# Interleaving the wo and w4 projections, and their loads, with the last batch's PV in a decode-attention kernel

## Chip, cores, metric

One core of one Trainium2 chip. The metric is the device time of one execution in microseconds. The kernel before takes 239.89 us (median of 4 runs, 239.72 to 240.89). Profiled spans start and end inside that time: the run profiled for the kernel before has a span of 238.0 us.

The engines are PE (TensorE, matmuls), PEld (its weight loads), DVE (VectorE), ACT (ScalarE), POOL (GpSimd) and SP (SyncE, which issues the loads here). The granted clock is the share of TensorE's full clock that it was given. PV is the product of the softmax weights and V; wo, w3 and w4 stand for the matmuls with these weights. A hand-over is the time in which PE waits until DVE has copied a result that PE's next matmuls read.

## The reference, cut to what matters

```python
def reference(A_x, A_k_cache, A_v_cache, A_wq, A_wo, B_x, B_w1, B_w2, B_w3, B_w4):
    x = A_x                                     # 4 x 1 x 576
    xn = _layernorm(x)
    return x + attention(xn, ...) + mixer_mlp(xn, ...)

# attention: 4 batches, 32 query heads on 16 K/V heads, the last 2048 of 8192 keys, head size 128
    q = xn @ wq;  p = softmax(q k^T * Dh**-0.5);  o = p v;   return o @ wo     # wo: 4096 x 576
# mixer_mlp with one token: its shifted groups are all padding, so x1 = xn
    h2 = gelu(layernorm(xn) @ w3) @ w4;         return xn + h2                 # w3: 576 x 4608, w4: 4608 x 576
```

About three quarters of the traffic is K and V, 32 loads of 1 MB for each of the two; the four weights add some 20 MB. 87.17 MB are read in all.

## The kernel before

K is transposed on TensorE, scores are built from 2-column matmuls, and PV runs in batches of four K/V heads: 16 accumulating matmuls of 512 columns. A "group" is two heads, one V load. The last batch, b = 3, holds groups 24 to 31. The parts that the change touches:

```python
def pe_PVbatch(b, gg):                      # 16 matmuls, 128x512, into one of two PSUM banks
    n = b * NPB + gg
    for G in range(pr0 // GP, (pr0 + PVB) // GP):
        PE.wait(("vld", G))                 # both V groups have landed
    ...
def pv_evac(b, gg):                         # DVE: four 128x128 evictions, scaled by 1/sum
    ...
def pe_oTacc(b, gg):                        # PE: transposing matmuls, 128 columns, all heads accumulate
    PE.op(... e.matmul(out=misc[:, OTF:OTF + 128], lhsT=otmp[:, j, :], rhs=imask[:, j, :], start=first, stop=last))
# ... cut
for g in range(NGB):                        # groups of a batch, here as they run for the last one
    dma_kv("v", b * NGB + g)
    if ((g + 1) * GP) % PVB == 0:
        gg = ((g + 1) * GP) // PVB - 1
        if gg >= 1:
            pe_oTacc(b, gg - 1)
        pe_PVbatch(b, gg)
        pv_evac(b, gg)
    if not nxt:
        for j in w3_after.get(g, []):       # w3 blocks 0..3 in groups 0, 2, 4, 6
            dma_w3(j)
            pe_h2T(j)
pe_oTacc(b, NPB - 1)
DVE.op(... e.tensor_copy(out=oT_sb[..., b], in_=misc[:, OTF:OTF + HQ]))
# ... after the last batch
for i in range(len(w4_blocks)):             # blocks of 10, 9, 9, 5, 2, 1 chunks
    dma_w4(i)
for h in range(HQ):                         # wo: 32 heads x 5 matmuls of 4 columns
    ...
for i, (region, f0, n) in enumerate(w4_blocks):
    PE.wait(("w4", i))
    for fc in range(f0, f0 + n):            # w4: 36 chunks x 5 matmuls of 4 columns
        # the last of the five reads 64 columns into the next chunk, so it must have landed too
        if REM > 0 and fc + 1 < FC and w4_blocks[blk_of_fc[fc + 1]][0] == region:
            PE.wait(("w4", blk_of_fc[fc + 1]))
        ...
```

All loads go out from one queue (SyncE's), in program order; PE runs in program order as well.

## Time and profile before

| | before |
|---|---|
| median time | 239.89 us |
| profiled span | 238.0 us |
| last V group landed, PV starts | 215.6 us |
| last transfer ends | about 229 us |
| last w4 matmul done | 234.4 us |

The prediction below shows the page's slices, the chain and the timeline. One more view is useful for the comparison: what PE waited for from 183 us on, in the kernel before (engine, line, what it waited for: us in total, times, longest).

```profile
PE ktp L564 <- DMA wA<-in_B_w_dram: 5.3, 4, 1.9
PE pvb_ps L512 <- DMA v_ring<-in_A_v_cache_dram: 3.2, 4, 1.0
...
PE st_ps L702 <- issue: 1.2, 2, 0.8
...
PE st_ps L687 <- DVE oT_sb L672: 0.3, 1, 0.3
```

PE waits for transfers in small pieces, up to the last V group. After it no wait is for a transfer. DVE is listed with one wait of 0.3 us ahead of wo, but the way from the end of PV (221.94) to wo (223.71) took 1.8 us in all, with DVE's evictions and PE's transposing matmuls in turn. A line such as L687 names where in the code the instruction comes from (wo); L702 is w4, L564 is w3, L512 is PV.

### The profile page before, as it was taken

How to read it: one execution, taken by the hardware profiler on the slowest of the kernel's cores; microseconds unless marked ns; L12 is line 12 of the kernel's file. 1: busy time of each engine (PE TensorE's matmuls, PEld its weight loads, DVE VectorE, ACT ScalarE, POOL GpSimd, SP SyncE). 2: the span in 40 equal slices, each digit the busy share in tenths (PEclk: the TensorE clock that was granted, in tenths of full speed). 3: DMA queues.
4: the chain of work that ended last, by engine and by line, in shares of the span. 5: the costliest groups of instructions: out<-in, count | busy, mean ns of one | idle time of the engine just before them, and what ended most of it. 6: DMA issues, size and time to landing. Idle time of an engine off the chain costs nothing.

```text
span 238.0 us, 6574 instructions
## 1 busy us (share of the span) xinstructions
PE 193.9 (81%) x3071; PEld 149.0 (63%) x3075; DVE 86.1 (36%) x195; ACT 63.8 (27%) x67; POOL 5.4 (2%) x9
## 2 busy tenths in 40 slices
PE   0499697779999697799998859999893758688884
PEld 0399597676867566767866557867662433333583
DVE  4444234542644426533644442635435010110200
ACT  8135143532423331333423043324313000000000
POOL 8000000000000000000000000000000000000000
PEclk9999769956999997799999957999999597675755
DMA  5999999999999999999999999999999999999910
GB/s 192 381 372 379 392 356 395 409 410 407 405 409 408 400 407 408 409 406 408 412 405 398 412 405 410 409 406 410 399 394 338 378 350 351 368 340 358 367 60 4
DMA packets 31240, 87.61 MB, mean 368 GB/s; under 512 B 1496, under 2 KB 10220, under 8 KB 31212
## 3 DMA queue, kind: packets, MB, share of 16 engines
q1 hardware_dynamic: 31212, 87.19, 96.7%
q8 instruction: 24, 0.39, 0.7%
q14 instruction: 4, 0.03, 0.0%
HBM read 87.17 MB, written 0.00 MB: 366 GB/s over the span
## 4 chain that ended last, share of the span: by engine, by line
PE 47%; DMA 34%; SPq 8%; DVE 7%; issue 2%; ACT 1%
PE ktp L440 18%; PE pvb_ps L512 15%; DMA k_ring<-in_A_k_cache_dram 14%; DMA v_ring<-in_A_v_cache_dram 12%; SPq L265 8%; DMA wA<-in_A_wq_dram 7%; PE st_ps L481 5%; DVE otmp L528 2%; PE st_ps L702 2%; DVE kt_sb L453 2%; PE st_ps L687 2%; PE misc_ps L549 2%; DVE part_sb L642 1%; ACT kt_sb L458 1%; DVE pm_sb L604 1%
## 5 line engine op out<-in xcount | busy, mean ns | idle before, releaser
L440 PE MATMUL ktp<-ident_bf,k_ring 128*128 128x128 bf16 x1024 | 89.1, 239 | 5.7 <-DMA k_ring<-in_A_k_cache_dram 3.7
L458 ACT ACTIVATE kt_sb<-ktp 128x1024 bf16<-128x1024 bf16 x51 | 52.1, 1023 | 93.5 <-PE ktp L440 93.5
L440 PEld LDWEIGHTS ktp<-ident_bf,k_ring 128*128 128x128 bf16 x1024 | 69.5, 108 | 8.5 <-DMA k_ring<-in_A_k_cache_dram 4.2
L512 PE MATMUL pvb_ps<-v_ring,pT_sb 128*128 128x512 bf16 x256 | 67.0, 421 | 3.2 <-DMA v_ring<-in_A_v_cache_dram 3.2
L453 DVE COPY kt_sb<-ktp 128x1024 bf16<-128x1024 bf16 x77 | 52.4, 690 | 42.4 <-PE ktp L440 42.3
L512 PEld LDWEIGHTS pvb_ps<-v_ring,pT_sb 128*128 128x128 bf16 x256 | 26.3, 106 | 37.3 <-issue 16.3
L481 PE MATMUL st_ps<-qT_sb,kt_sb 128*128 128x2 bf16 x1024 | 44.6, 165 | 1.8 <-ACT kt_sb L458 1.4
L528 DVE TENSOR_SCALAR otmp<-pvb_ps,rrs 128x128 bf16<-128x128 f32 x64 | 18.0, 343 | 75.7 <-PE pvb_ps L512 75.7
L481 PEld LDWEIGHTS st_ps<-qT_sb,kt_sb 128*128 128x128 bf16 x1024 | 40.4, 99 | 4.0 <-ACT kt_sb L458 1.7
L564 PE MATMUL ktp<-uT_sb,wA 128*128 128x4 bf16 x180 | 5.3, 165 | 5.3 <-DMA wA<-in_B_w_dram 5.3
L549 PE MATMUL misc_ps<-imask,otmp 128*128 128x128 bf16 x64 | 8.7, 231 | 1.0 <-DVE otmp L528 0.4
L564 PEld LDWEIGHTS ktp<-uT_sb,wA 128*128 128x128 bf16 x180 | 5.0, 100 | 6.8 <-DMA wA<-in_B_w_dram 6.3
L613 ACT ACTIVATE pT_sb<-st_ps 128x512 bf16<-128x512 f32 x4 | 2.4, 597 | 24.8 <-PE ktp L440 17.7
L569 ACT ACTIVATE gT_sb<-ktp 128x36 bf16<-128x36 f32 x4 | 0.8, 200 | 30.0 <-PE ktp L564 30.0
L645 PE MATMUL misc_ps<-ones_f,part_sb 128*128 128x1 f32 x8 | 2.1, 337 | 7.3 <-DVE part_sb L642 7.3
L336 PE MATMUL misc_ps<-ident_bf,xn_pad 128*128 128x128 bf16 x5 | 0.7, 302 | 7.6 <-DVE xn_pad L319 7.6
L549 PEld LDWEIGHTS misc_ps<-imask,otmp 128*128 128x128 bf16 x64 | 4.5, 100 | 3.4 <-DVE otmp L528 3.4
L645 PEld LDWEIGHTS misc_ps<-ones_f,part_sb 128*128 128x128 f32 x8 | 1.8, 280 | 6.8 <-DVE part_sb L642 6.8
L336 PEld LDWEIGHTS misc_ps<-ident_bf,xn_pad 128*128 128x128 bf16 x5 | 0.5, 130 | 7.5 <-issue 7.5
L702 PE MATMUL st_ps<-gT_sb,k_ring 128*128 128x4 bf16 x140 | 4.2, 166 | 1.2 <-issue 1.2
L702 PEld LDWEIGHTS st_ps<-gT_sb,k_ring 128*128 128x128 bf16 x140 | 4.0, 104 | 1.4 <-issue 1.4
L687 PE MATMUL st_ps<-oT_sb,wo_sb 128*128 128x4 bf16 x160 | 4.4, 166 | 0.3 <-DVE oT_sb L672 0.3
(68 smaller groups left out, 51.6 us busy)
## 6 DMA issues: line engine op xcount, KB each, us to landing
k_ring<-in_A_k_cache_dram SPq DMA_DIRECT2D x32, 1024.0 KB, 15.2
v_ring<-in_A_v_cache_dram SPq DMA_DIRECT2D x32, 1024.0 KB, 16.9
wo_sb<-in_A_wo_dram SPq DMA_DIRECT2D x4, 1152.0 KB, 19.2
wA<-in_B_w_dram SPq DMA_DIRECT2D x4, 1152.0 KB, 16.1
wA<-in_A_wq_dram SPq DMA_DIRECT2D x4, 1024.0 KB, 12.1
k_ring<-in_B_w_dram SPq DMA_DIRECT2D x2, 1296.0 KB, 16.3
k_ring<-in_B_w_dram SPq DMA_DIRECT2D x1, 1440.0 KB, 19.2
kt_sb<-in_B_w_dram SPq DMA_DIRECT2D x1, 720.0 KB, 11.2
```

What stands on the lines that cost most here:

```text
L265: DQ.ops.append(("op", lambda e, o=out_ap, i=in_ap, s=s: e.dma_start(o, i).then_inc(s, 16), False))
L440: PE.op(lambda e, tt=tt, t=t, src=src, bank=bank: e.transpose(out=bank[:, tt * 128:(tt + 1) * 128], in_=src[:, t * 128:(t + 1) * 128], ide ...
L453: DVE.op(lambda e: e.tensor_copy(out=dst, in_=src), mark=("evac", c))
L458: ACT.op(lambda e: e.activation(out=dst, in_=src, func=ACTF.Copy), mark=("evac", c))
L481: PE.op(lambda e, t=t, src=src, hl0=hl0, b=b, stb=stb, st0=(first_of_b and tt == 0): e.matmul(out=stb[:, t * HL + hl0:t * HL + hl0 + REP], ...
L512: PE.op(lambda e, t=t, vs0=vs0, bank=bank: e.matmul(out=bank[:, 0:PVB * 128], lhsT=pT_sb[:, t, :], rhs=v_ring[:, vs0:vs0 + PVB, t * 128:(t ...
L528: DVE.op(lambda e, jj=jj, j=j, bank=bank: e.tensor_scalar(out=otmp[:, j, :], in0=bank[:, jj * 128:(jj + 1) * 128], scalar1=rrs32[:, 0:1], ...
L549: PE.op(lambda e, j=j, first=first, last=last: e.matmul(out=misc[:, OTF:OTF + 128], lhsT=otmp[:, j, :], rhs=imask[:, j, :], start=first, s ...
L564: PE.op(lambda e, ff=ff, fc=fc, dc=dc, bank=bank: e.matmul(out=bank[:, ff * B:(ff + 1) * B], lhsT=wA[:, dc, fc * 128:(fc + 1) * 128], rhs= ...
L645: PE.op(lambda e: e.matmul(out=misc[:, RSC:RSC + 1], lhsT=part_sb[:, :], rhs=ones_f[:, 0:1], start=True, stop=True), mark=("rs", b))
L687: PE.op(lambda e, h=h, dc=dc, c0=c0: e.matmul(out=accT[:, dc * B:(dc + 1) * B], lhsT=wo_sb[:, h * D + c0:h * D + c0 + 128], rhs=oT_sb[:, h ...
L702: PE.op(lambda e, fc=fc, dc=dc, c0=c0, last=last: e.matmul(out=accT[:, dc * B:(dc + 1) * B], lhsT=w4_chunk(fc, c0, 128), rhs=gT_sb[:, fc * ...
```

## The change

The intent: while the last batch still waits for V, PE should already do the wo matmuls of finished heads and the w4 matmuls. For this the oT matmuls write only the columns of their own heads, with one DVE copy per PV batch; the last PV batch of four heads is split into two halves; the loads of w4 are moved up between V groups; and x's load and half of the output go out from ACT's queue.

```diff
+    for b_ in range(B):
+        for gg_ in range(NPB):
+            if b_ == B - 1 and gg_ == NPB - 1 and PVB > GP:
+                for k_ in range(PVB // GP):
+                    PVBATCH.append((b_, gg_ * PVB + k_ * GP, GP))      # two half batches
+            else:
+                PVBATCH.append((b_, gg_ * PVB, PVB))
...
+        act_dma(x_sb[:, :], A_x.rearrange("b s d -> (b s) d"), s_x, key="x")
...
+        def pe_oTacc(n):
+            for jj in range(npr):
+                PE.op(... out=misc[:, OTF + c0:OTF + c1], lhsT=otmp[:, j, :], rhs=imask[:, j, c0:c1],
+                    start=(jj == 0), stop=(jj == npr - 1)) ...
+            DVE.op(... e.tensor_copy(out=oT_sb[...][:, c0:c1, b], in_=misc[:, OTF + c0:OTF + c1]), mark=("oTb", n))
...
+                extra = [("w3", j) for j in range(NWB)] + [("w4", i) for i in range(len(w4_blocks))]
+                n_tail = max(1, min(3, len(w4_blocks) - 1))
+                mid = extra[:len(extra) - n_tail]       # w3 x4, w4[10], w4[9], w4[9]: one in each of groups 0..6
+                tail = extra[len(extra) - n_tail:]      # w4[5], w4[2], w4[1]
...
+                for g in range(NGB):
+                    dma_kv("v", b * NGB + g)
+                    for n in batches:
+                        if (j0 + npr) == (g + 1) * GP:
+                            pe_PVbatch(n)
+                            pv_evac(n)
+                            flush_pending()             # oT matmuls and wo of the batch before
+                            pending.append(n)
+                    for item in per_g.get(g, []):
+                        do_extra(item)                  # load w3/w4 block, then its matmuls
+                for k, item in enumerate(tail):
+                    if k == 1 or k == len(tail) - 1:
+                        flush_pending()
+                    do_extra(item)
-        for i in range(len(w4_blocks)):
-            dma_w4(i)
-        for h in range(HQ):  ...                        # wo, then w4, after everything
...
-            tiny_dma(out2[:, NFULL * 128:D], out20[NFULL * B:NR, 0:REM], s_out)
+            ACT.wait("fin")
+            act_dma(out2[:, NFULL * 128:D], out20[NFULL * B:NR, 0:REM], s_out)
```

More of the change, by code (lines that the diff above doesn't have):

```diff
@@ L110, in bass_parallel_sum__sliding_block_cached__mixer_s_mlp__decode_kernel @@
     NPB = HKV // PVB
+    PVBATCH = []
+    for b_ in range(B):
[5 more added lines that the diff above has]
+                PVBATCH.append((b_, gg_ * PVB, PVB))
+    PVB_OF_B = {b_: [n_ for n_, (bb_, _, _) in enumerate(PVBATCH) if bb_ == b_] for b_ in range(B)}
     TPC = min(8, NT)
@@ L267, in bass_parallel_sum__sliding_block_cached__mixer_s_mlp__decode_kernel, with act_dma @@
         tiny_dma = sp_dma
+        def act_dma(out_ap, in_ap, s, key=None):
+            dma_counts[s.num] = dma_counts.get(s.num, 0) + 1
+            if key is not None:
+                EV[key] = (s, 16 * dma_counts[s.num])
+            ACT.ops.append(("op", lambda e, o=out_ap, i=in_ap, s=s: e.dma_start(o, i).then_inc(s, 16), False))
+        act_dma(x_sb[:, :], A_x.rearrange("b s d -> (b s) d"), s_x, key="x")
         DVE.op(lambda e: e.memset(ones_bf[:, :], 1.0), mark="ones")
@@ L350, in bass_parallel_sum__sliding_block_cached__mixer_s_mlp__decode_kernel @@
             mark="xT")
-        tiny_dma(x_sb[:, :], A_x.rearrange("b s d -> (b s) d"), s_x, key="x")
         def dma_wq(j):
@@ L494, in k_drain, with pe_PVbatch @@
                 pe_QK(c)
-        def pe_PVbatch(b, gg):
-            n = b * NPB + gg
-            pr0 = b * HKV + gg * PVB
+        def pe_PVbatch(n):
+            b, j0, npr = PVBATCH[n]
+            pr0 = b * HKV + j0
             vs0 = pr0 % NVS
+            assert vs0 + npr <= NVS
             bank = pvb[n % 2]
-            for G in range(pr0 // GP, (pr0 + PVB) // GP):
+            groups = list(range(pr0 // GP, (pr0 + npr) // GP))
+            for G in groups:
                 PE.wait(("vld", G))
             if n >= 2:
-                for jj in range(PVB):
-                    PE.wait(("otmp", n - 2, jj))
+                PE.wait(("otmp", n - 2))
             for t in range(NT):
@@ L508, in pe_PVbatch @@
                 if t == NT - 1:
-                    marks = [("pvb", n)] + [("vfree", G) for G in range(pr0 // GP, (pr0 + PVB) // GP)]
-                    if gg == NPB - 1:
-                        marks.append(("pv", b))
-                PE.op(lambda e, t=t, vs0=vs0, bank=bank: e.matmul(
-                    out=bank[:, 0:PVB * 128], lhsT=pT_sb[:, t, :],
-                    rhs=v_ring[:, vs0:vs0 + PVB, t * 128:(t + 1) * 128], start=(t == 0), stop=(t == NT - 1)),
+                    marks = [("pvb", n)] + [("vfree", G) for G in groups]
@@ L515, in pe_PVbatch, with pv_evac @@
+                PE.op(lambda e, t=t, vs0=vs0, npr=npr, bank=bank: e.matmul(
+                    out=bank[:, 0:npr * 128], lhsT=pT_sb[:, t, :],
+                    rhs=v_ring[:, vs0:vs0 + npr, t * 128:(t + 1) * 128], start=(t == 0), stop=(t == NT - 1)),
                     mark=marks)
-        def pv_evac(b, gg):
-            n = b * NPB + gg
+        def pv_evac(n):
+            b, j0, npr = PVBATCH[n]
             bank = pvb[n % 2]
-            for jj in range(PVB):
-                j = gg * PVB + jj
-                eng = DVE
-                eng.wait(("pvb", n))
-                eng.wait(("rrs", b))
-                if b >= 1:
-                    eng.wait(("oTacc", b - 1, gg))
-                if eng is DVE:
-                    DVE.op(lambda e, jj=jj, j=j, bank=bank: e.tensor_scalar(
-                        out=otmp[:, j, :], in0=bank[:, jj * 128:(jj + 1) * 128], scalar1=rrs32[:, 0:1],
-                        scalar2=None, op0=ALU.mult), mark=("otmp", n, jj))
-                else:
-                    ACT.op(lambda e, jj=jj, j=j, bank=bank: e.activation(
-                        out=otmp[:, j, :], in_=bank[:, jj * 128:(jj + 1) * 128], func=ACTF.Copy,
-                        scale=rrs32[:, 0:1]), mark=("otmp", n, jj))
@@ L536, in pe_oTacc @@
-        def pe_oTacc(b, gg):
-            n = b * NPB + gg
-            PE.wait("imask")
-            for jj in range(PVB):
-                j = gg * PVB + jj
-                PE.wait(("otmp", n, jj))
-                first = (gg == 0 and jj == 0)
-                last = (gg == NPB - 1 and jj == PVB - 1)
-                marks = None
-                if jj == PVB - 1:
-                    marks = [("oTacc", b, gg)]
-                    if last:
-                        marks.append(("oTp", b))
-                PE.op(lambda e, j=j, first=first, last=last: e.matmul(
-                    out=misc[:, OTF:OTF + 128], lhsT=otmp[:, j, :], rhs=imask[:, j, :], start=first, stop=last),
-                    mark=marks)
+            DVE.wait(("pvb", n))
@@ new lines, in pv_evac @@
+            DVE.wait(("rrs", b))
+            prev = [m for m in PVB_OF_B.get(b - 1, []) if PVBATCH[m][1] < j0 + npr and PVBATCH[m][1] + PVBATCH[m][2] > j0]
+            for m in prev:
+                DVE.wait(("oTacc", m))
+            for jj in range(npr):
+                j = j0 + jj
+                DVE.op(lambda e, jj=jj, j=j, bank=bank: e.tensor_scalar(
+                    out=otmp[:, j, :], in0=bank[:, jj * 128:(jj + 1) * 128], scalar1=rrs32[:, 0:1],
+                    scalar2=None, op0=ALU.mult), mark=(("otmp", n) if jj == npr - 1 else None))
@@ new lines, in pe_oTacc @@
+        def pe_oTacc(n):
+            b, j0, npr = PVBATCH[n]
+            c0, c1 = j0 * REP, (j0 + npr) * REP
+            PE.wait("imask")
+            PE.wait(("otmp", n))
+            if n >= 1:
+                PE.wait(("oTb", n - 1))
+            for jj in range(npr):
+                j = j0 + jj
+                PE.op(lambda e, j=j, jj=jj, c0=c0, c1=c1, npr=npr: e.matmul(
+                    out=misc[:, OTF + c0:OTF + c1], lhsT=otmp[:, j, :], rhs=imask[:, j, c0:c1],
+                    start=(jj == 0), stop=(jj == npr - 1)),
+                    mark=(("oTacc", n) if jj == npr - 1 else None))
+            DVE.wait(("oTacc", n))
+            DVE.op(lambda e, b=b, c0=c0, c1=c1: e.tensor_copy(
+                out=oT_sb[:, :].rearrange("p (h b) -> p h b", b=B)[:, c0:c1, b], in_=misc[:, OTF + c0:OTF + c1]),
+                mark=("oTb", n))
@@ new lines, in bass_parallel_sum__sliding_block_cached__mixer_s_mlp__decode_kernel, with pe_wo @@
+        acc_started = [False]
+        def pe_wo(h0, h1):
+            PE.wait("dmem")
+            for h in range(h0, h1):
+                PE.wait(("wo", h // HPW))
+                if REM > 0 and h + 1 < HQ:
+                    PE.wait(("wo", (h + 1) // HPW))
+                for dc, (c0, rows) in enumerate(DCH):
+                    st0 = not acc_started[0]
+                    acc_started[0] = True
+                    PE.op(lambda e, h=h, dc=dc, c0=c0, st0=st0: e.matmul(
+                        out=accT[:, dc * B:(dc + 1) * B], lhsT=wo_sb[:, h * D + c0:h * D + c0 + 128],
+                        rhs=oT_sb[:, h * B:(h + 1) * B], start=st0, stop=False, skip_group_check=True))
@@ new lines, in bass_parallel_sum__sliding_block_cached__mixer_s_mlp__decode_kernel, with pe_w4mm @@
+        blk_of_fc = {}
+        for i_, (region_, f0_, n_) in enumerate(w4_blocks):
+            for fc_ in range(f0_, f0_ + n_):
+                blk_of_fc[fc_] = i_
+        def pe_w4mm(i, last_block):
+            region, f0, n = w4_blocks[i]
+            PE.wait(("w4", i))
+            for fc in range(f0, f0 + n):
+                PE.wait(("gelu", fc // FPB))
+                if REM > 0 and fc + 1 < FC and w4_blocks[blk_of_fc[fc + 1]][0] == region:
+                    PE.wait(("w4", blk_of_fc[fc + 1]))
+                for dc, (c0, rows) in enumerate(DCH):
+                    last = (last_block and fc == f0 + n - 1 and dc == NDC - 1)
+                    st0 = not acc_started[0]
+                    acc_started[0] = True
+                    PE.op(lambda e, fc=fc, dc=dc, c0=c0, last=last, st0=st0: e.matmul(
+                        out=accT[:, dc * B:(dc + 1) * B], lhsT=w4_chunk(fc, c0, 128),
+                        rhs=gT_sb[:, fc * B:(fc + 1) * B], start=st0, stop=last, skip_group_check=True),
+                        mark=("acc" if last else None))
@@ L592, in bass_parallel_sum__sliding_block_cached__mixer_s_mlp__decode_kernel @@
         k_drain(0, CPB)
-        w3_after = {}
-        if NWB > 0:
-            for j in range(NWB):
-                g = min(NGB - 1, (j * NGB) // NWB)
-                w3_after.setdefault(g, []).append(j)
         for b in range(B):
@@ L649, in bass_parallel_sum__sliding_block_cached__mixer_s_mlp__decode_kernel @@
             PE.wait(("exp", b))
-            for g in range(NGB):
-                if nxt and g > 0:
-                    dma_kv("k", (b + 1) * NGB + g)
-                    for c in range(c1_lo + g * CPG, c1_lo + (g + 1) * CPG):
-                        k_items(c, c1_lo)
-                dma_kv("v", b * NGB + g)
-                if ((g + 1) * GP) % PVB == 0:
-                    gg = ((g + 1) * GP) // PVB - 1
-                    if gg >= 1:
-                        pe_oTacc(b, gg - 1)
-                    pe_PVbatch(b, gg)
-                    pv_evac(b, gg)
-                if not nxt:
-                    for j in w3_after.get(g, []):
-                        if j == 0:
-                            DQ.wait(("q", NQB - 1))
-                        dma_w3(j)
-                        pe_h2T(j)
@@ L668, in bass_parallel_sum__sliding_block_cached__mixer_s_mlp__decode_kernel @@
-            if nxt:
-                k_drain(c1_lo, c1_lo + CPB)
-            pe_oTacc(b, NPB - 1)
-            DVE.wait(("oTp", b))
-            DVE.op(lambda e, b=b: e.tensor_copy(
-                out=oT_sb[:, :].rearrange("p (h b) -> p h b", b=B)[:, :, b], in_=misc[:, OTF:OTF + HQ]),
-                mark=("oT", b))
-        DQ.wait(("kfree", NP // GP - 1))
-        DQ.wait(("qkall", B - 1))
-        for i in range(len(w4_blocks)):
-            dma_w4(i)
-        PE.wait(("oT", B - 1))
-        PE.wait("dmem")
@@ L682, in bass_parallel_sum__sliding_block_cached__mixer_s_mlp__decode_kernel @@
-        for h in range(HQ):
-            PE.wait(("wo", h // HPW))
-            if REM > 0 and h + 1 < HQ:
-                PE.wait(("wo", (h + 1) // HPW))
-            for dc, (c0, rows) in enumerate(DCH):
-                PE.op(lambda e, h=h, dc=dc, c0=c0: e.matmul(
-                    out=accT[:, dc * B:(dc + 1) * B], lhsT=wo_sb[:, h * D + c0:h * D + c0 + 128],
-                    rhs=oT_sb[:, h * B:(h + 1) * B], start=(h == 0 and dc == 0), stop=False, skip_group_check=True))
-        blk_of_fc = {}
@@ L691, in bass_parallel_sum__sliding_block_cached__mixer_s_mlp__decode_kernel @@
-        for i, (region, f0, n) in enumerate(w4_blocks):
-            for fc in range(f0, f0 + n):
-                blk_of_fc[fc] = i
-        for i, (region, f0, n) in enumerate(w4_blocks):
-            PE.wait(("w4", i))
-            for fc in range(f0, f0 + n):
-                PE.wait(("gelu", fc // FPB))
-                if REM > 0 and fc + 1 < FC and w4_blocks[blk_of_fc[fc + 1]][0] == region:
-                    PE.wait(("w4", blk_of_fc[fc + 1]))
-                for dc, (c0, rows) in enumerate(DCH):
-                    last = (fc == FC - 1 and dc == NDC - 1)
-                    PE.op(lambda e, fc=fc, dc=dc, c0=c0, last=last: e.matmul(
-                        out=accT[:, dc * B:(dc + 1) * B], lhsT=w4_chunk(fc, c0, 128),
-                        rhs=gT_sb[:, fc * B:(fc + 1) * B], start=False, stop=last, skip_group_check=True),
-                        mark=("acc" if last else None))
+            batches = PVB_OF_B[b]
@@ new lines, in bass_parallel_sum__sliding_block_cached__mixer_s_mlp__decode_kernel, with do_extra, flush_pending @@
+            pending = []
+            if nxt:
+                for g in range(NGB):
+                    if g > 0:
+                        dma_kv("k", (b + 1) * NGB + g)
+                        for c in range(c1_lo + g * CPG, c1_lo + (g + 1) * CPG):
+                            k_items(c, c1_lo)
+                    dma_kv("v", b * NGB + g)
+                    for n in batches:
+                        _, j0, npr = PVBATCH[n]
+                        if (j0 + npr) == (g + 1) * GP:
+                            for m in pending:
+                                pe_oTacc(m)
+                            pending = []
+                            pe_PVbatch(n)
+                            pv_evac(n)
+                            pending.append(n)
+                k_drain(c1_lo, c1_lo + CPB)
+                for m in pending:
+                    pe_oTacc(m)
+            else:
+                extra = [("w3", j) for j in range(NWB)] + [("w4", i) for i in range(len(w4_blocks))]
+                n_tail = max(1, min(3, len(w4_blocks) - 1))
+                mid = extra[:len(extra) - n_tail]
+                tail = extra[len(extra) - n_tail:]
+                per_g = {}
+                for k, item in enumerate(mid):
+                    gslot = min(NGB - 1, (k * NGB) // max(1, len(mid)))
+                    per_g.setdefault(gslot, []).append(item)
+                w3_started = [False]
+                def do_extra(item):
+                    kind, idx = item
+                    if kind == "w3":
+                        if not w3_started[0]:
+                            DQ.wait(("q", NQB - 1))
+                            w3_started[0] = True
+                        dma_w3(idx)
+                        pe_h2T(idx)
+                    else:
+                        if idx == 0:
+                            DQ.wait(("kfree", NP // GP - 1))
+                            DQ.wait(("qkall", B - 1))
+                        dma_w4(idx)
+                        pe_w4mm(idx, idx == len(w4_blocks) - 1)
+                def flush_pending():
+                    for m in pending:
+                        pe_oTacc(m)
+                        _, j0, npr = PVBATCH[m]
+                        PE.wait(("oTb", m))
+                        pe_wo(j0 * REP, (j0 + npr) * REP)
+                    del pending[:]
+                for g in range(NGB):
+                    dma_kv("v", b * NGB + g)
+                    for n in batches:
+                        _, j0, npr = PVBATCH[n]
+                        if (j0 + npr) == (g + 1) * GP:
+                            pe_PVbatch(n)
+                            pv_evac(n)
+                            flush_pending()
+                            pending.append(n)
+                    for item in per_g.get(g, []):
[4 more added lines that the diff above has]
+                    do_extra(item)
+                assert not pending
```

## The prediction

> **What bounds the kernel now.** I read the page first. Its slices say that two things bound this kernel in turn: transfers up to about 228 us, then a tail that is all TensorE.
>
> ```profile
> PE   0499697779999697799998859999893758688884
> PEclk9999769956999997799999957999999597675755
> DMA  5999999999999999999999999999999999999910
> ```
>
> A slice is 5.95 us. DMA is at 9 in 37 of 40 slices, while PE still has 8884 in the last four. So everything before 228 us is paced by the 87.17 MB that are read, and the change does not touch that number. The chain that ended last then shows what the tail is made of (start us, length us, what):
>
> ```profile
> 215.65 6.29 PE pvb_ps L512 x16
> ...
> 223.42 0.24 DVE oT_sb L672
> 223.71 4.37 PE st_ps L687 x160
> 228.24 0.78 issue
> 229.02 3.54 PE st_ps L702 x127
> ```
>
> The last PV batch starts when the last V group has landed (215.65), and wo (160 matmuls) and w4 (180) come strictly after it. The accumulator is complete at 234.4 and the span ends at 238.0, so 3.6 us are the epilogue. Small windows of 1 us show where the transfers stop (window, length, PE, PEld, DVE, ACT, POOL, then clock, DMA share, GB/s):
>
> ```profile
> 225.00:226.00 1.00, 1.00 (x44) 1.00 (x42) 0.00 (x0) 0.00 (x0) 0.00 (x0) 0.50 0.83 297
> 228.00:229.00 1.00, 0.24 (x9) 0.15 (x6) 0.00 (x0) 0.00 (x0) 0.00 (x0) 0.50 0.09 31
> 229.00:230.00 1.00, 0.98 (x36) 0.98 (x37) 0.00 (x0) 0.00 (x0) 0.00 (x0) 0.50 0.00 0
> ```
>
> The last bytes land at about 229.0, with some of the engines done 3 to 4 us before the slowest. If PE could keep up, the end would be near 229 + 0.2 + 3.6 = 233. That is the gain the change is after, about 5 us. Whether PE can keep up is read from the timeline of the last stage (start, length, engine, line, what, idle before and releaser):
>
> ```profile
> 206.16 5.91 PE L512 MATMUL pvb_ps<-v_ring,pT_sb 128*128 128x512 bf16 x16 [0.63 <-DMA v_ring<-in_A_v_cache_dram]
> 212.11 1.13 DVE L528 TENSOR_SCALAR otmp<-pvb_ps,rrs 128x128 bf16<-128x128 f32 x4 [9.02 <-PE pvb_ps L512]
> 213.20 1.29 PE L564 MATMUL ktp<-uT_sb,wA 128*128 128x4 bf16 x45 [1.13 <-DMA wA<-in_B_w_dram]
> 215.65 6.28 PE L512 MATMUL pvb_ps<-v_ring,pT_sb 128*128 128x512 bf16 x16 [0.71 <-DMA v_ring<-in_A_v_cache_dram]
> ```
>
> A PV batch costs 5.2 to 6.3 us here (5.21, 5.30, 5.91, 6.28), against 3.45 in the middle of the kernel, because its first matmuls are 427 ns apart at a granted clock of 0.50. Each of these starts also marks a landing, since it waits for a DMA: V groups 25, 27, 29, 31 at 187.1, 196.6, 206.2, 215.6; w3 blocks 1 to 3 at 194.2, 203.7, 213.2.
>
> **What the Trainium skill says.** "TensorE: Matmul & The Clock Gate", Part 1, has the clock at half until a free-running window of 3.4 us was busy. The trace agrees: 0.50 and 1.00 in stretches of about 3.4 us, PV at half clock first. It also shows that 4-column matmuls do not count: PE is 1.00 busy from 224 to 228 with wo and the clock stays at 0.50. "DMA: Bandwidth & Descriptors", section "Issuing engines are not separate DMA queues", says that issuing from a second engine saves only issue time; so moving x and half of the output to ACT can buy no bandwidth. "Runtime: NRT & Kernel Launch", section "Instruction fetch mechanics", has instructions refilled in blocks of 256; the 0.78 us of "issue" stands exactly 127 matmuls with their weight loads before the next gap (0.42 us), so I take both for refills that did not come in time.
>
> **The change part by part.**
>
> 1. *x on ACT.* The first wq transfer moves up from 1.21 to 0.80 us, so the whole stream by 0.4: its end goes from 229.0 to 228.6. LayerNorm starts a little later behind ACT, which the wait for wq and K hides.
>
> 2. *Narrow oT matmuls.* 8 columns in place of 128, with a DVE copy each batch. Batches 0 to 2 are paced by transfers: nothing.
>
> 3. *The order of the loads.* Before: v24 w3 v25 v26 w3 v27 v28 w3 v29 v30 w3 v31, then all of w4 (10, 9, 9, 5, 2, 1 chunks). After: v24 w3 v25 w3 v26 w3 v27 w3 v28 w4[10] v29 w4[9] v30 w4[9] v31 w4[5,2,1]. So V groups 27 to 31 arrive later. Backwards from 228.6: w4 took 229.0 - 215.65 = 13.3 us for 36 chunks, 0.37 each. The last 8 chunks take 3.0, so v31 lands at 225.6; a V group takes about 2.5 (215.65 - 213.20), nine chunks 3.3: third w4 block 223.1, v30 219.8, second w4 block 217.3, v29 214.0. v31 is 10 us later than before.
>
> 4. *The order on PE, and a wait in it.* The listing of PE's queue shows that the last chunk of the first w4 block waits for the second w4 block (its 128 columns reach into the next chunk), and that stands ahead of the third PV batch. So this batch starts not at 214.0 but at 217.3, after PE sat idle and cold for some 5 us.
>
> 5. *PE from there*, all dense and in program order:
>  - PV of groups 28, 29: 5.7 (middle of the four).
>  - Flush of the previous batch: DVE does four evictions (1.13) before the oT copy (0.2), with hand-overs 1.5; then 40 wo matmuls at 27.3 ns (4.37 us / 160) 1.1. Together 2.6.
>  - w4[9]: 45 x 27.7 ns = 1.25.
>  - PV half batch: 16 x 213 ns (half of 427, clock still low after 4 us of small matmuls) = 3.4. Flush with two evictions 0.9 + 1.1 = 2.0. w4[9] 1.25.
>  - PV half batch 3.4; flush 0.9 + 20 matmuls 0.55 = 1.45; w4[5] 0.7; last flush 0.5 + 0.55; w4[2,1] 0.4.
>  - Change-overs and waits on PE, about 0.3.
>
>  Sum 5.7 + 2.6 + 1.25 + 3.4 + 2.0 + 1.25 + 3.4 + 1.45 + 0.7 + 1.05 + 0.4 + 0.3 = 23.5. The accumulator is complete at 217.3 + 23.5 = 240.8, against 234.4.
>
> 6. *The output split over SP and ACT.* The second issue no longer waits for the first (0.6 to 0.7): epilogue 3.0.
>
> Span 240.8 + 3.0 = 243.8, by the middle values; 5.8 longer than 238.0. I take half a microsecond off, because the DVE copy is now of 8 columns and no refill gap should be left where PV matmuls stand between: 243.3. The median time lies 1.9 above the profiled span (239.89 against 238.0): 245.2 us.
>
> In one sentence: the change moves 2.3 us of small matmuls (90 of 340) ahead of the critical start, but it moves a whole PV batch of 5.7 us behind it and puts four serial DVE hand-overs on PE's path.
>
> **The rivals.**
>
> *PE keeps up and DMA sets the end.* Then the time is about 233 + 1.9 - 1 = 234. For it: PE is only some 80% busy in the last 50 us, and the intent is sound. Against it: after v31 lands at 225.6 there are only 3 us of transfers, while one half batch of PV alone takes 3.4; even without the wait of step 4, PV of 28, 29 starts at 214.0 and the sum ends at 237.5, still 240 as a span and 242 as a time.
>
> *The clock stays up.* Denser PE work could leave the clock at 1.00: PV 4.7 and twice 1.8, some 4 us less, time 241. Against it: the wo and w4 matmuls between do not lift the clock, and each flush holds PE still for 0.9 to 1.5 us.
>
> *Worse waits.* A V group that waits for its buffer, or DVE late with a copy, would add 2 to 3 us: 248. Against it: the transfers are issued some 16 us ahead of landing, and groups 24, 25 are free at about 192.
>
> **Range and chances.** The two terms that carry the most doubt are the landing of the second w4 block (1 us either way) and the clock in three PV pieces (the window's phase differs from run to run, up to 1.5 us); flushes add 0.5. That makes 241.8 to 247.8. The limit for "slower by over 2%" is 244.7, half a microsecond under my value, so the odds are near even: 0.57 slower, 0.39 within, 0.04 faster, the last for the case that I misread the order.
>
> **What would show it.** Right: transfers end at 228 to 229 while PE runs on to 240; the third PV batch starts near 217 after an idle PE, released by w4 and not by V; the half batches take 3.4 us each at a clock of 0.50; before each wo group PE waits 1 to 1.5 us for the oT copy; the epilogue is near 3.0. Wrong: PV at full clock in the tail, w4[9] landing before 215, or a last matmul within 2 us of the last byte.

## The result, and the profile after

The changed kernel takes 243.46 us (median of 11 runs, 241.89 to 246.5) against 239.8 us for the kernel before in the same rounds. The ratio is 1.0155, with a 95% interval of 1.012 to 1.0189: slower, but within the 2% line. Two of the eleven runs (246.5 and 246.47) are classed slow, being over 1.5% above the fastest; the ratio leaves them out. A ratio here is the mean time of one kernel's fast runs over that of the other's of the same rounds, so it is not quite the ratio of the medians. The fast runs of the changed kernel scatter by 3.6 us (4.6 with the two slow ones), the runs of the kernel before by 2.4.

The page's slices of the changed kernel (a slice is 6.06 us):

```profile
PE   0399679769979686999789669999863917529784
PEclk9999797979999997999999758999995785956977
DMA  7999999999999999999999999999999999999500
```

DMA is full to slice 37 (38 before) and half full in the next; then two empty slices follow, and PE has a 1 and a 2 (slices 33 and 36) ahead of its last busy stretch. The chain of the changed kernel shows the same in time (start us, length us, what):

```profile
206.28 12.18 DMA k_ring<-in_B_w_dram
218.46 0.14 issue
218.60 0.28 PE st_ps L594 x5
218.87 5.24 PE pvb_ps L526 x16
224.11 0.03 issue
224.14 1.12 DVE otmp L541 x4
...
225.40 1.16 PE st_ps L574 x40
226.56 1.13 PE st_ps L594 x45
227.68 1.78 PE pvb_ps L526 x16
...
230.24 1.15 PE st_ps L574 x40
231.39 1.13 PE st_ps L594 x45
232.52 3.31 PE pvb_ps L526 x16
...
239.27 0.19 DVE accT_sb L764
```

The third PV batch does not wait for V: five w4 matmuls ahead of it wait for a w4 load ("k_ring<-in_B_w_dram" is w4's second block) until 218.60. From there to 239.2 the chain is PE, with DVE between. The same is read from PE's waits after 183 us:

```profile
PE st_ps L594 <- DMA k_ring<-in_B_w_dram: 6.3, 2, 4.6
...
PE st_ps L574 <- DVE oT_sb L559: 4.2, 5, 1.2
```

Both lines are new: w4's wait, 4.6 us at once, and five hand-overs to DVE with 4.2 us in all. One of the five lies ahead of the third batch. From the end of PV work to wo the other four cost 1.3, 0.8, 0.8 and 0.3 us in the chain, 3.2 us, against the 1.8 us of the kernel before. Windows of 1 us (window, length, PE, PEld, DVE, ACT, POOL, clock, DMA share, GB/s) show the idle PE in the middle of the transfers and the end of them:

```profile
216.00:217.00 1.00, 0.00 (x0) 0.00 (x0) 0.00 (x0) 0.00 (x0) 0.00 (x0) 0.50 1.10 416
...
228.00:229.00 1.00, 1.00 (x12) 0.90 (x10) 0.00 (x0) 0.00 (x0) 0.00 (x0) 1.00 0.44 140
229.00:230.00 1.00, 0.53 (x9) 0.40 (x6) 0.51 (x2) 0.00 (x0) 0.00 (x0) 1.00 0.05 18
230.00:231.00 1.00, 0.76 (x30) 0.77 (x31) 0.18 (x2) 0.00 (x0) 0.00 (x0) 1.00 0.00 0
```

The transfers end just after 229 us (at about 229 before); PE's last w4 matmul ends 10 us later, where before it ended 5 us later.

### The profile page after: what moved, and what is told of

The parts are those of the page before. It is cut to its first block, busy times and chain, and to the rows that moved or that the text cites.

```text
span 242.5 us, 6618 instructions
## 1 busy us (share of the span) xinstructions
PE 184.4 (76%) x3087; PEld 145.9 (60%) x3091; DVE 87.2 (36%) x208; ACT 63.8 (26%) x67; POOL 5.4 (2%) x9
## 4 chain that ended last, share of the span: by engine, by line
DMA 44%; PE 37%; SPq 7%; DVE 6%; ACT 3%; issue 1%; ACTq 0%
DMA k_ring<-in_A_k_cache_dram 28%; PE pvb_ps L526 14%; PE ktp L455 14%; SPq L274 7%; DMA wA<-in_A_wq_dram 6%; DMA v_ring<-in_A_v_cache_dram 6%; DMA k_ring<-in_B_w_dram 5%; PE st_ps L496 4%; DVE otmp L541 3%; PE st_ps L574 1%; PE st_ps L594 1%; DVE kt_sb L468 1%; PE st_ps L427 1%; ACT wA L299 1%; ACT L331 1%
## 5 line engine op out<-in xcount | busy, mean ns | idle before, releaser
L455 PE MATMUL ktp<-ident_bf,k_ring 128*128 128x128 bf16 x1024 | 86.9, 236 | 8.4 <-DMA k_ring<-in_A_k_cache_dram 7.9
L455 PEld LDWEIGHTS ktp<-ident_bf,k_ring 128*128 128x128 bf16 x1024 | 67.5, 106 | 11.4 <-DMA k_ring<-in_A_k_cache_dram 8.5
L526 PE MATMUL pvb_ps<-v_ring,pT_sb 128*128 128x512 bf16 (+1 forms) x272 | 64.7, 397 | 2.9 <-DMA v_ring<-in_A_v_cache_dram 2.9
L526 PEld LDWEIGHTS pvb_ps<-v_ring,pT_sb 128*128 128x128 bf16 x272 | 27.3, 105 | 32.6 <-issue 9.8
L496 PEld LDWEIGHTS st_ps<-qT_sb,kt_sb 128*128 128x128 bf16 x1024 | 39.9, 99 | 4.7 <-ACT kt_sb L473 2.4
L574 PEld LDWEIGHTS st_ps<-oT_sb,wo_sb 128*128 128x128 bf16 x160 | 4.3, 96 | 4.6 <-DVE oT_sb L559 4.6
L554 PE MATMUL misc_ps<-imask,otmp 128*128 128x8 bf16 (+1 forms) x64 | 4.1, 168 | 2.5 <-DVE otmp L541 2.5
```

The lines of the kernel that those rows point to most:

```text
L455: PE.op(lambda e, tt=tt, t=t, src=src, bank=bank: e.transpose(out=bank[:, tt * 128:(tt + 1) * 128], in_=src[:, t * 128:(t + 1) * 128], ide ...
L496: PE.op(lambda e, t=t, src=src, hl0=hl0, b=b, stb=stb, st0=(first_of_b and tt == 0): e.matmul(out=stb[:, t * HL + hl0:t * HL + hl0 + REP], ...
L526: PE.op(lambda e, t=t, vs0=vs0, npr=npr, bank=bank: e.matmul(out=bank[:, 0:npr * 128], lhsT=pT_sb[:, t, :], rhs=v_ring[:, vs0:vs0 + npr, t ...
L554: PE.op(lambda e, j=j, jj=jj, c0=c0, c1=c1, npr=npr: e.matmul(out=misc[:, OTF + c0:OTF + c1], lhsT=otmp[:, j, :], rhs=imask[:, j, c0:c1], ...
L574: PE.op(lambda e, h=h, dc=dc, c0=c0, st0=st0: e.matmul(out=accT[:, dc * B:(dc + 1) * B], lhsT=wo_sb[:, h * D + c0:h * D + c0 + 128], rhs=o ...
```

## The experiments

Theory A is the prediction's: V groups 28 to 31 arrive later because w3 and w4 loads were put ahead of them, and a w4 wait stands ahead of a PV batch. The rival, theory B: the order of the loads is harmless, and the added hand-overs and half batches make the loss. All runs gave correct results. The first four ran on one chip, with the kernel before at 240.04 us beside them.

| run | what | median us | ratio to before, 95% |
|---|---|---|---|
| e3 | before, only the new order of loads | 248.92 | 1.0366 (1.0335 to 1.0397) |
| e2 | changed, w4's loads last again | 235.45 | 0.9818 (0.9783 to 0.9853) |
| e1 | changed, w4 matmuls behind the next PV | 243.61 | 1.0156 (1.012 to 1.0192) |
| e4 | changed, flush behind the w4 matmuls | 242.84 | 1.0094 (1.0048 to 1.0141) |
| e5 | changed kernel again | 246.16 | 1.0228 (1.0175 to 1.028) |
| e6 | changed, with idle matmuls for the clock | 243.73 | 1.0129 (1.0089 to 1.017) |
| e7 | e1 with idle matmuls | 241.01 | 1.0032 (1.0007 to 1.0056) |
| e8 | before, only ACT's two transfers | 239.09 | 0.9963 (0.9943 to 0.9982) |
| e12 | e2 again | 236.13 | 0.9837 (0.9795 to 0.9879) |
| e9 | e2, oT copy ahead of the evictions | 235.05 | 0.9795 (0.9756 to 0.9835) |
| e10 | e9 with w3 in groups 0 to 3 | 235.34 | 0.9818 (0.9771 to 0.9865) |
| e11 | e2 without half batches | 235.72 | 0.9821 (0.9776 to 0.9865) |

At the 2% line e3 is slower and e1, e4, e6, e7 and e8 are the same; e2, e5 and e9 to e12 are unclear, because their intervals cross it.

### e3: only the order of the loads

```diff
 # kernel before
-                g = min(NGB - 1, (j * NGB) // NWB)
+                g = j
...
+                    if NWB <= g < NWB + 3:
+                        dma_w4(g - NWB)          # in the group loop; PE's order unchanged
...
-        for i in range(len(w4_blocks)):
+        for i in range(3, len(w4_blocks)):
             dma_w4(i)
```

> The kernel before with only its loads in the new order (w3 in groups 0 to 3, w4's three large blocks between the last V groups); PE's work as before, wo and w4 at the end. Theory A: V group 31 lands near 226.5, the last PV batch (6 us), eviction and oT (1.7), wo (4.4) and w4 (5 to 6) follow it: end of the accumulator near 244.5, time 250 us, 10 us above before. Theory B: no hand-overs were added, so the time stays at 240 us.

248.92 us, 8.9 above before, with no instruction added on PE or DVE. The chain of this run:

```profile
212.72 14.05 DMA v_ring<-in_A_v_cache_dram
226.77 0.14 issue
226.90 5.16 PE pvb_ps L512 x16
...
233.83 4.22 PE st_ps L690 x160
238.05 3.55 PE st_ps L705 x133
```

The last PV batch starts at 226.9 and not at 215.65; wo and w4 follow it as they did. Theory A's number came out (226.5 and 250 were expected), theory B's did not (240). This is the direct cost of the order of the loads.

### e2 and e12: everything but the order of the loads

```diff
 # changed kernel
-                n_tail = max(1, min(3, len(w4_blocks) - 1))
+                n_tail = len(w4_blocks)          # w3 back in groups 0, 2, 4, 6; all w4 behind the last V
```

> The changed kernel with the old order of loads: all w4 loads behind the last V group, w3 in groups 0, 2, 4, 6; the wo interleave, the half batches, the hand-overs and ACT's two transfers are kept. Theory A: V group 31 lands near 216, PE is through with PV and wo by 221 to 224 and then eats w4 as it lands; transfers end near 229.5, span 233, time 235 us (2% faster than before). Theory B: all hand-overs are still there, so little is won: 241 to 243 us.

235.45 us, 1.8% faster than before. The timeline of e2 (start, length, engine, line, what):

```profile
204.93 6.10 PE L526 MATMUL pvb_ps<-v_ring,pT_sb 128*128 128x512 bf16 x16 [0.39 <-DMA v_ring<-in_A_v_cache_dram]
...
213.34 3.55 PE L526 MATMUL pvb_ps<-v_ring,pT_sb 128*128 128x256 bf16 x16
...
219.84 3.24 PE L526 MATMUL pvb_ps<-v_ring,pT_sb 128*128 128x256 bf16 x16
...
228.96 1.21 PE L594 MATMUL st_ps<-gT_sb,kt_sb 128*128 128x4 bf16 x40
```

The third batch starts at 204.9 (218.7 in the changed kernel), all of PV is over at 223, and w4 runs to 230.2. From 205 us on PE no longer waits for any transfer in this profile; its last bytes land near 228, so PE still sets the end. All hand-overs are still in it, so theory B falls: by themselves they do not make the loss. ACT's two transfers are in it as well; e8 below puts them at 0.9 us, so an estimate for the interleaving alone is 4.6 - 0.9 = 3.7 us.

> The kernel of run e2 again, as the base for the three beside it on the same chip: 235.5 us, 1.8% faster than before.

It was run again as the base for e9 to e11: 236.13 us, 0.9837. The gain holds.

### e1: the w4 wait alone

```diff
 # changed kernel: a large w4 block's matmuls are kept back until behind the next PV batch and its flush
                         dma_w4(idx)
-                        pe_w4mm(idx, idx == len(w4_blocks) - 1)
+                        if idx < len(mid) - NWB:
+                            late.append(idx)
+                        else:
+                            pe_w4mm(idx, idx == len(w4_blocks) - 1)
...
                             pending.append(n)
+                            for i_ in late:
+                                pe_w4mm(i_, False)
+                            del late[:]
```

> The changed kernel with one thing moved: PE's matmuls on the three large w4 blocks come behind the next PV batch, so that no w4 wait stands ahead of a PV batch; loads as in the changed kernel. Theory A (PV inputs late, and a w4 wait ahead of the third PV batch): the batch starts when V group 29 has landed, near 215 instead of 218.7, but 45 w4 matmuls (1.25 us) that were done in the idle time now follow it: net 2.5 us earlier, time 241 us, still above before. Theory B (the hand-overs to DVE and the half batches make the loss, not the order of the loads): the wait is idle time that costs little, time within 0.5 us of the changed kernel, 243.5 us.

In its profile the wait is gone and the batch starts when V has landed:

```profile
214.04 5.68 PE L526 MATMUL pvb_ps<-v_ring,pT_sb 128*128 128x512 bf16 x16 [4.20 <-DMA v_ring<-in_A_v_cache_dram]
```

That profiled run was 241.41 us (span 239.6, 2.9 less than the changed kernel's). But the median of the six runs was 243.61, where 241 was expected: no better than the changed kernel's 243.46 of another set. By this run alone the question stayed open. The other five runs had granted clocks of 0.834 to 0.863 over the span, the profiled one 0.870.

### e5, e6, e7: the same chip, and the clock held up

> The changed kernel as it is, on the same chip as the runs beside it, since moving the w4 wait (run e1) gave 2.9 us in its profile and nothing in the median of its timed runs, where the granted clock was lower (0.83 to 0.86 against 0.85 to 0.88). If chips or chance made that, this kernel's median on this chip lies near 244.5 to 246, 1.5 to 2.5 us above e1's. If e1 really wins nothing, it is 243.5 again.

The changed kernel run again, beside e6 and e7: 246.16 us, ratio 1.0228. So one kernel measured 1.0155 in one set and 1.0228 in another; the intervals hardly touch. Against the fastest run of the first set (241.89), four of these six runs lie over 1.5% higher; the other two took 243.97. Against 246.16, e1's 243.61 is 2.5 us better, as expected, but on another chip, and the first set speaks against it. The profile of this run shows where its extra time lies (its span is 243.9):

```profile
217.45 6.50 PE L526 MATMUL pvb_ps<-v_ring,pT_sb 128*128 128x512 bf16 x16
...
227.44 3.21 PE L526 MATMUL pvb_ps<-v_ring,pT_sb 128*128 128x256 bf16 x16
...
233.59 3.55 PE L526 MATMUL pvb_ps<-v_ring,pT_sb 128*128 128x256 bf16 x16
```

In the first profile these three took 5.37, 1.91 and 3.45 us, in this one 6.50, 3.21 and 3.55: 2.5 us more on PV alone. The same instructions differ by the granted clock: from 225 to 230 us it was 1.00 in the first profile and 0.67 in this one.

e6 and e7 add matmuls whose results nobody reads, to keep the clock up:

```diff
+        def pe_warm(k):                           # 128x512, into a PSUM bank that is free by then
+            for _ in range(k):
+                PE.op(lambda e: e.matmul(out=ktp_f[1][:, 0:512], lhsT=ident_bf[:, :], rhs=identrep[:, :], start=True, stop=True))
 # e6: changed kernel; e7: e1
+   10 ahead of the w4 wait (e7: 9 ahead of the third PV batch); 5 or 3 in each wait for DVE; 3 between wo and w4, twice
```

> The changed kernel with idle work: 128x512 matmuls into an unused bank, 10 ahead of the w4 wait, 5 or 3 in each wait for DVE, 3 between wo and w4 twice (these six cost 1.3 us at full clock). Results are unchanged. Clock theory: the scatter of 242 to 246.5 and some 3 us of the tail are matmuls at half clock: PV 3.5 instead of 5.4, half batches 1.8 each instead of 1.9 to 3.4; net of the 1.3 us some 2.5 us faster, 241 us, and the runs agree within 1.5 us. If the clock is not what scatters, the kernel gets 1 to 2 us slower, 245 us.

> Run e1 (w4 matmuls behind the next PV batch) with the same idle work, 9 of the 128x512 matmuls ahead of the third PV batch. With the clock held up in both, the w4 wait alone is left as the difference to the kernel beside it: 2.5 us less, 238.5 us. If the wait cost nothing, equal to it.

e6 took 243.73 us, 2.4 less than e5 beside it although it does more, and its runs span 2.0 us (e5's 3.0). But it is no faster than the first set of the changed kernel (243.46). The PV of its profile:

```profile
218.50 3.66 PE L526 MATMUL pvb_ps<-v_ring,pT_sb 128*128 128x512 bf16 x16
...
226.25 1.91 PE L526 MATMUL pvb_ps<-v_ring,pT_sb 128*128 128x256 bf16 x16
...
231.74 3.09 PE L526 MATMUL pvb_ps<-v_ring,pT_sb 128*128 128x256 bf16 x16
```

The three take 8.66 us here, against 13.26 in e5's profile and 10.73 in the first. So half clock costs PV some microseconds in the profiles: that much is shown. What holding the clock up is worth in time is open, since e5's set was slower than the first. I had expected 241; the last half batch still ran partly at half clock.

The third batch of e7's profile:

```profile
214.90 5.25 PE L526 MATMUL pvb_ps<-v_ring,pT_sb 128*128 128x512 bf16 x16 [2.75 <-DMA v_ring<-in_A_v_cache_dram]
```

e7 took 241.01 us, 2.7 below e6 on the same chip, and the intervals of the two ratios do not touch. The difference expected was 2.5; the time itself was expected at 238.5 and missed by 2.5. It is the best measure of the w4 wait here, though not of the wait alone, since the idle matmuls differ too: in e7 nine of them end at 212.2, PE then waits 2.75 us for V, and the batch takes 5.25 us (3.66 in e6). With both half batches at 1.91 us, PV takes 9.07 us in all, 0.4 more than in e6, so a faster PV does not make the gain. It fits what e1's profile showed. Why e1's median showed nothing, and why whole sets of runs of one kernel differ by 1%, is not settled. The mean clock of a run does not order the times: in the first set the run at 0.881 took 244.39 us and one at 0.849 took 243.12.

### e4 and e9: the hand-overs to DVE

```diff
 # e4: changed kernel, flush behind the group's w3/w4 matmuls
                             pv_evac(n)
-                            flush_pending()
-                            pending.append(n)
+                            fresh.append(n)
                     for item in per_g.get(g, []):
                         do_extra(item)
+                    if fresh:
+                        flush_pending()
+                        pending.extend(fresh)
```

> The changed kernel with the flush (oT and wo matmuls of the previous batch) behind the w3 or w4 matmuls of the group instead of ahead of them, so that DVE's evictions pass beside PE's w4 work. Theory A counts these hand-overs as 1.2, 0.7 and 0.7 us of waiting in the tail (three of the four): up to 2.5 us less, time 241 us. If PE is not what sets the end, no change: 243.5 us.

e4 took 242.84 us (one of its six runs is slow): 3.3 below e5 and 0.6 below the first set of the changed kernel. The direction is the expected one, but the intervals of e4 and the first set overlap, and the two sets of the changed kernel lie 2.7 us apart, so this is inconclusive. The cleaner test has its base on the same chip:

```diff
 # e9: e2, DVE's copy for the old batch ahead of the evictions of the new one
-                            pv_evac(n)
                             flush_pending()
+                            pv_evac(n)
                             pending.append(n)
```

> Run e2 with DVE's order turned: the oT copy of the previous batch ahead of the four (or two) evictions of the new one, so that PE waits 0.3 us for it and not 1.2 (0.7). In e2's profile PE is dense from 212 us to the end at 230.2, while the last bytes land at 227.6, so PE sets the end by 2.5 us: three hand-overs less 0.9 + 0.4 + 0.4 make 1.5 us, time 234 us. If the transfers set the end, no gain: 235.5 us.

e9 took 235.05 us, 1.1 below e12 (1.5 were expected); the ratios' intervals overlap, so this is a hint and no proof. PE's waits for the copy fell to 0.27 us, and now it waits for transfers again up to the end:

```profile
211.25 1.15 PE L574 MATMUL st_ps<-oT_sb,wo_sb 128*128 128x4 bf16 x40 [0.27 <-DVE oT_sb L559]
...
226.06 1.47 PE L594 MATMUL st_ps<-gT_sb,k_ring 128*128 128x4 bf16 x50 [1.04 <-DMA k_ring<-in_B_w_dram]
227.85 1.56 PE L594 MATMUL st_ps<-gT_sb,kt_sb 128*128 128x4 bf16 x40 [0.32 <-DMA kt_sb<-in_B_w_dram]
```

That is the state that the change was after: PE ends with the last bytes. e9 beats both kernels, by 2.1% against before (interval 1.7 to 2.4%, so whether it is over 2% is unclear).

### e10 and e11: w3 first, and no half batches

```diff
 # e10: e9 with
-                    gslot = min(NGB - 1, (k * NGB) // max(1, len(mid)))
+                    gslot = k
 # e11: e2 with PVBATCH never split
```

> Run e9 with w3 in groups 0 to 3 as in the changed kernel, w4 still last: V groups 28 to 31 land one behind the other up to 215, and PE has no w3 matmuls left in the tail (1.3 us less there), but it gets the third PV batch some 4 us later. Theory: 234 us like e9, within 1 us; if a late third PV batch alone costs what it cost in the changed kernel, 237 us or more.

> Run e2 with the last PV batch whole instead of in two halves. The halves let one half of PV start when group 30 has landed, 2.5 us before 31, but cost one more hand-over; without them PV starts at 215, takes 6 us, and PE's work ends near 230.5 as in e2. Theory: 235.5 us, within 1 us of e2, the split is worth nothing here. If the split carries e2's gain, 238 us or more.

e10 took 235.34 and e11 235.72 us, both within noise of e9 and e12. e10 has its third PV batch 4 us later than e9 (210.3 against 206.0) at no cost that these runs resolve. A likely reason, argued and not shown, is slack: in its profile e9 waits 2.6 us for w4's loads, and in e10's (of its slowest run, 236.79) no such wait is left. So moving w3 costs nothing that shows; w4 ahead of V is what costs. The half batches are worth nothing that shows with the loads in this order; with V late, as in the changed kernel, they were not tested.

### e8: ACT's two transfers alone

```diff
 # kernel before
-        tiny_dma(x_sb[:, :], ..., s_x, key="x")            # first on SyncE's queue
+        act_dma(x_sb[:, :], ..., s_x, key="x")             # on ACT's queue
...
-            tiny_dma(out2[:, NFULL * 128:D], ...)
+            ACT.wait("fin")
+            act_dma(out2[:, NFULL * 128:D], ...)
```

> The kernel before with x's load and the second half of the output on ACT's queue, nothing else. Prediction: 0.4 us earlier start of the stream and 0.3 to 0.6 us less at the end, 239.2 us against 240.0. Rival: x lands later (3.1 instead of 2.3 us in the profiles) and PE starts 0.6 us later, which eats the gain: 240 us.

239.09 against 240.18 us, ratio 0.9963: 0.9 us by the ratio (1.1 between the medians), about the size predicted. But not by the way predicted at the start. The windows 0 to 5 and 5 to 10 us, first of the kernel before, then of e8:

```profile
0.00:5.00 5.00, 0.00 (x0) 0.00 (x0) 2.47 (x14) 4.18 (x3) 4.01 (x9) 1.00 0.48 156
5.00:10.00 5.00, 0.98 (x8) 0.75 (x9) 2.76 (x9) 1.97 (x4) 1.38 (x1) 1.00 1.00 376
```

```profile
0.00:5.00 5.00, 0.00 (x0) 0.00 (x0) 2.47 (x14) 3.57 (x3) 4.00 (x9) 1.00 0.57 183
5.00:10.00 5.00, 0.69 (x5) 0.46 (x5) 2.43 (x8) 2.57 (x4) 1.40 (x1) 1.00 1.02 354
```

In 10 us that is 2.66 MB before and 2.69 MB after (5 us x the GB/s, added), under 0.1 us of lead. At 5 us e8 is ahead by 0.14 MB, worth the 0.4 us that were expected (at 376 GB/s), and from 5 to 10 us it loses that again. The epilogue fell from 3.6 to 3.3 us. What makes the rest of the 0.9 is open.

## Why the prediction was right

The time, 243.46 in the first set and 246.16 in the second, lies in the range of 241.8 to 247.8 on both sides of the 245.2 predicted, and the mechanism is the predicted one. Part of the nearness is luck. In the first profile the critical start came 1.3 us late and PE's work from there was 2.9 us short, and half a microsecond had been taken off for reasons that were not measured; so the span came out at 242.5, where 243.3 was predicted. The range is not quite what its terms give: 1, 1.5 and 0.5 us around 245.2 make 242.2 to 248.2, which holds both results too. Point by point:

- **Order of the loads.** Shown by e3 and e2. Alone it costs 8.9 us; the rest of the change alone gains 4.6. The two add up to +4.3, between the +3.7 and the +6.0 measured for the whole in its two sets (differences of medians). That they add is not shown: the w4 wait exists only where both are together.
- **The w4 wait ahead of the third batch.** PE waited 4.6 us, released by w4, predicted "some 5". The batch was expected behind a landing at 217.3; the landing came at 218.5 in one profile and 217.2 in the other.
- **PE's sum from there.** Predicted 23.5 us. In the two profiles of the changed kernel: 239.2 - 218.6 = 20.6, and 240.5 - 217.3 = 23.2. More than half of what was missing in the first is the first half batch, 1.8 us where 3.4 stood, since the clock had stayed at 1.00; the hand-overs (0.6) and the first batch (0.5) make most of the rest. That the clock would be low there every time was the failing step: it was low in one of the two profiles. In the first profile the clock was 1.00 from 222.3 to 232.5, then 0.50 to 236.0: the first half batch fell into the high stretch, and the second began as that stretch ended. That this makes the scatter of the timed runs is likely, but not shown.
- **Hand-overs.** Predicted 1.5, 0.9 and 0.9 us from the end of PV to wo; the chain shows 225.40 - 224.11 = 1.3, and 230.24 - 229.46 = 0.8 for a half batch (it ended at 227.68 + 1.78). Right, a little too high. No refill gap was expected between PV matmuls, and none is in the chain.
- **ACT's transfers.** The step "the whole stream by 0.4 earlier" failed: transfers end just after 229, no earlier than before, and e8 has lost its lead by 10 us. The epilogue fell to 3.2 us, where 3.0 was said.
- **The chances.** 0.57 for slower by over 2% and 0.39 for within: the first set fell within, at 1.0155, the second just outside, at 1.0228. Near even was a fair account.
- **The rivals.** PE did not keep up; that it can is shown by e9, with another order of loads. The clock that stays up exists in part (e6). No buffer wait appeared.

## What to carry to other kernels

When transfers set the pace, the order of loads is a schedule for the compute engine. In this kernel what feeds the longest remaining compute (V, with 5 to 6 us of PV behind each pair of groups) had to land first, and what feeds the shortest (w4, 1.3 us a block) last; try that order first elsewhere. Interleaving compute was a gain of its own, and should be tried without moving the loads. In an in-order engine, look for a wait on a later load ahead of work whose data have landed.

## What the Trainium skill lacked or had wrong

- "TensorE: Matmul & The Clock Gate", Part 1, gives one busy window of about 3.4 us as the condition for the full clock, and doesn't say whether small matmuls count as busy. Here they did not: in the kernel before, wo's 4-column matmuls fill PE to 1.00 from 224 to 228 us, the clock falls to 0.50 at 224.5, and it is still at 0.50 in every later window to the end.
- "DMA: Bandwidth & Descriptors", section "Why a DMA increments its semaphore by 16 and not by 1", has the engines finish independently, but gives no size. At the end of the stream here the mean DMA share falls over 4 us (0.83 at 225 us to 0.09 at 228 us before), which fits engines that finish up to 4 us apart. The view gives only their mean, so this is argued, here and in the prediction.
- "Runtime: NRT & Kernel Launch", section "Instruction fetch mechanics", calls the crossing of a 256-instruction block mostly hidden. The dense small matmuls of the kernel before show gaps of 0.78 and 0.42 us, 127 matmuls and as many weight loads apart (254 instructions), that nothing else in the profile explains. The gaps keep to their places in the program: e8's profile has one of 1.72 us behind the same 6 w4 matmuls and none later, e3's has only the second, 0.40 us behind 133. That fits refills, but no run tested it.
